# Sliding-window attention with global tokens and a top-k mixture of experts: blocks of 64 queries, heads in quads, grouped selection, one-hot inversion

## The chip, the cores and the metric

The kernel is one program on one core of a Trainium2 chip. Its time is the device time of one launch in microseconds (us). The kernel before took 876.09 us, the median of three runs (876.02, 876.09, 879.5).

The engines have their names from the profile: PE is TensorE, DVE is VectorE, ACT is ScalarE, POOL is GpSimd, SP is SyncE. POOL and SP also issue DMA transfers. The profile gives TensorE's granted clock as a share of full speed; its two levels are 0.5 (1.2 GHz) and 1.0 (2.4 GHz).

## The reference

Attention runs over 8 batches of 8 heads with 512 local and 32 global tokens and a head size of 64. Global queries see every token. A local query sees the 32 globals and the local keys at most 32 places away. The 4352 rows of 512 that come out go through a mixture of 8 experts: each row goes to its best expert, each expert keeps its 80 rows of highest gate, and every other row of the output is zero.

```python
out_g = softmax(scale * q_g @ k_all.T) @ v_all                     # global queries
s_ll  = where(abs(i - j) <= 32, scale * q_l @ k_l.T, -1e9)         # band
out_l = softmax(concat(scale * q_l @ k_g.T, s_ll)) @ concat(v_g, v_l)
x = concat(out_g, out_l) as (8 * 544, 512)
e = argmax(x @ w_gate);  gate = softmax(x @ w_gate)[e]
for each expert e: keep the 80 rows of e with the highest gate
    out[rows] = gate[rows] * (relu(x[rows] @ w1[e]) @ w2[e])       # 512 -> 1024 -> 512
```

## The kernel before

It has four stages, one after another.

**Attention, batch by batch, in pairs of heads.** Queries and keys come as fp16 by ten DMAs a batch on POOL's queue (L156 to L160), values as fp32 on SP's (L162). A pair is transposed on PE (L189, L191), copied by ACT (L194, L195), scored in blocks of 128 keys by 192 queries (L205; global queries L208, global keys L213, L215) and put through exp by ACT (L219 to L225). DVE multiplies by the band of zeros and ones (L227, 128x896 per head). In the product with the values, the 65 columns of a value block (64 and a column of ones for the denominator) are stationary, and the fp32 exponentials move through (L232, L235 for the globals; L240, L242): the result is `xTu`, 65 rows by tokens. It has to be turned round: ACT copies it (L247, L248), and PE multiplies it as the stationary operand with `wx`, an identity with the head's rows of the gate weights beside it (L251, L253). So `px` holds token rows, their denominators and their share of the gate logits; DVE divides and adds up (L256 to L272). Every fp32 matmul counts as two in the profile, a transpose as one.

**Selection.** After a batch its rows go to DRAM (`x_scr`, L277, L279). DVE makes gates and a one-hot score (L282 to L307), PE turns it to 8 experts x 640 tokens (L311), and ten rounds of MAX8 and MATCH_REPLACE (L318, L321) put the batch's 80 best per expert into `cand`. After the last batch ten more rounds over the 8x640 of `cand` (L332, L334) give each expert's threshold.

**Routing.** Every kept token gets its place, expert times 80 plus its rank among the kept (L337 to L401). 40 indirect DMAs on POOL's queue scatter token number and gate to those places in DRAM (`tokgate_scr`, L406).

**Experts.** For each expert: read back 80 numbers and gates (L416), gather 80 rows (L420), transpose (L424), first product with the rows stationary (L432), relu (L436, L437), transposes of the hidden rows (L442), second product (L448), gate (L451), scatter to the output (L453). The weights of experts 0 to 2 are loaded during attention; those of e+3 are issued on POOL's queue within expert e (L144, L146).

Each engine takes its instructions in the order of the program; a buffer in a pool is handed out again when its readers are done. `order` rows below show that order.

Of the kernel before, what the change touches and what calls it, by code (L numbers as in the profile page):

```python
# [18 lines left out]
P = 128  # L19
WIN = 32  # L20
QSTART = [0, 96, 224, 320]
NRND_B = 10
NRND_F = 10
WPREF = 3


def _np_consts(B, H, SL, SG, D, E, S, NT, cap):
    c = {}
    c["ident16"] = np.eye(P, dtype=np.float16)
    c["identf"] = np.eye(P, dtype=np.float32)  # L30
    m = np.zeros((P, 4, 224), dtype=np.float32)
    for j in range(4):
        p = np.arange(P)[:, None]
        col = np.arange(192)[None, :]
        q = QSTART[j] + col
        k = 128 * j + p
        m[:, j, 0:192] = (np.abs(q - k) <= WIN).astype(np.float32)
        m[:, j, 192:224] = 1.0
    c["band"] = m
    c["tri"] = (np.arange(P)[:, None] <= np.arange(P)[None, :]).astype(np.float32)  # L40
    tokid = np.full((P, NT), 2.0e9, dtype=np.float32)
    for b in range(B):
        for tau in range(4):
            tokid[:, b * 5 + tau] = b * S + SG + 128 * tau + np.arange(P)
        tokid[0:SG, b * 5 + 4] = b * S + np.arange(SG)
    c["tokid"] = tokid
    e80 = np.zeros((1, E, NT), dtype=np.float32)
    for e in range(E):
        e80[0, e, :] = e * cap
    c["e80"] = e80  # L50
    wxc = np.zeros((65, H, 73), dtype=np.float32)
    wxc[64, :, 8] = 1.0
    for h in range(H):
        wxc[0:64, h, 9:73] = np.eye(64, dtype=np.float32)
    c["wxc"] = wxc
    c["ones_row"] = np.ones((1, P), dtype=np.float32)
    return c
# [3 lines left out]
def kernel(  # L61
# [22 lines left out]
    NT = B * 5  # L84
    cap = int(moe_capacity)
    scale = float(1.0 / np.sqrt(D))
    assert SL == 512 and SG == 32 and D == 64 and P == 128 and DF == H * D

    c = _np_consts(B, H, SL, SG, D, E, S, NT, cap)
    ident16_d = nc.inline_tensor(c["ident16"], name="cident16")  # L90
    identf_d = nc.inline_tensor(c["identf"], name="cidentf")
    band_d = nc.inline_tensor(c["band"], name="cband")
    tri_d = nc.inline_tensor(c["tri"], name="ctri")
    tokid_d = nc.inline_tensor(c["tokid"], name="ctokid")
    e80_d = nc.inline_tensor(c["e80"], name="ce80")
    wxc_d = nc.inline_tensor(c["wxc"], name="cwxc")
    ones_row_d = nc.inline_tensor(c["ones_row"], name="cones_row")

    x_dram = nc.dram_tensor("x_scr", (N, DF), BF16, kind="Internal")
    tg_dram = nc.dram_tensor("tokgate_scr", (E * cap, 2), FP32, kind="Internal")  # L100

    cpool = ctx.enter_context(tc.tile_pool(name="consts", bufs=1))
    gpool = ctx.enter_context(tc.tile_pool(name="glob", bufs=1))
    wpool = ctx.enter_context(tc.tile_pool(name="wpool", bufs=WPREF))

    ident16 = cpool.tile([P, P], FP16, name="ident16")
    nc.sync.dma_start(out=ident16, in_=ident16_d.ap())
    identf = cpool.tile([P, P], FP32, name="identf")
    nc.sync.dma_start(out=identf, in_=identf_d.ap())
    identbf = cpool.tile([P, P], BF16, name="identbf")  # L110
    nc.gpsimd.dma_start(out=identbf, in_=identf_d.ap())
    band = cpool.tile([P, 4, 224], FP32, name="band")
    nc.sync.dma_start(out=band, in_=band_d.ap())
    tri = cpool.tile([P, P], BF16, name="tri")
    nc.gpsimd.dma_start(out=tri, in_=tri_d.ap())
    tokidt = cpool.tile([P, NT], FP32, name="tokidt")
    nc.sync.dma_start(out=tokidt, in_=tokid_d.ap())
    e80t = cpool.tile([1, E, NT], FP32, name="e80t")
    nc.sync.dma_start(out=e80t, in_=e80_d.ap())
    ones_row = cpool.tile([1, P], FP32, name="ones_row")  # L120
    nc.sync.dma_start(out=ones_row, in_=ones_row_d.ap())
    wx = cpool.tile([65, H, 73], FP32, name="wx")
    nc.sync.dma_start(out=wx, in_=wxc_d.ap())
    nc.sync.dma_start(out=wx[0:64, :, 0:8], in_=moe_w_gate.rearrange("(h d) e -> d h e", d=64))

    zt = gpool.tile([P, DF], FP32, name="zt")
    nc.vector.memset(zt, 0.0)
    out_t = out.rearrange("(t p) d -> t p d", p=P)
    ztg = gpool.tile([P, (E * cap // P) * 2], FP32, name="ztg")
    nc.vector.memset(ztg, 0.0)  # L130
    nc.sync.dma_start(out=tg_dram.ap().rearrange("(a p) c -> p a c", p=P), in_=ztg)

    score_all = gpool.tile([P, E, NT], FP32, name="score_all")
    gate_all = gpool.tile([P, NT], FP32, name="gate_all")
    nc.vector.memset(score_all, 0.0)
    nc.vector.memset(gate_all, 0.0)
    cand = gpool.tile([E, B, 8 * NRND_B], FP32, name="cand")

    w1sb = {}
    w2sb = {}  # L140
# [7 lines left out]
    with tc.tile_pool(name="battn", bufs=2) as bpool, \  # L148
# [4 lines left out]
        def load_batch(bb):  # L153
# [14 lines left out]
            bt[bb] = (qk16, qkg16, vb, vgb)  # L168

        load_batch(0)  # L170
        for b in range(B):
            if b + 1 < B:
                load_batch(b + 1)
            if b == 1:
# [315 lines left out]
```

## Time and profile before

| what | value |
|---|---|
| median of three runs | 876.09 us |
| profiled execution: span | 878.1 us |
| PE busy | 505.7 us, 58% |
| DVE busy | 326.9 us, 37% |
| ACT busy | 174.9 us, 20% |
| POOL busy | 134.2 us, 15% |
| DMA, mean | 58 GB/s |

The span of the profiled execution is taken as its own time; it is 2.0 us above the median of the runs. Busy shares are means over four stages with different limits, so a stage is read from its own window and from the chain of work that ended last.

### The profile page before, as it was taken

The numbers are of one execution on the slowest core, as the hardware profiler recorded it, in microseconds if no ns is written. First come the engines' busy times: TensorE is split into PE (matmuls) and PEld (weight loads), VectorE is DVE, ScalarE is ACT, GpSimd is POOL, SyncE is SP. The second block draws the span as 40 slices with busy tenths as digits, with TensorE's granted clock in tenths as the row PEclk, the third lists the DMA queues.
The fourth block names the chain that finished last, engine by engine and source line by source line (L and its number), as shares of the span: only waits on it lengthen the run. The fifth ranks groups of instructions, "written<-read, shape, count | busy, mean of one in ns | idle before, by whom it ended". The sixth has DMA issues, their size and how long they took to land.

```text
span 878.1 us, 8534 instructions
## 1 busy us (share of the span) xinstructions
PE 505.7 (58%) x3151; PEld 332.0 (38%) x3151; DVE 326.9 (37%) x1125; ACT 174.9 (20%) x441; POOL 134.2 (15%) x158
## 2 busy tenths in 40 slices
PE   0477868776886777788668688867401000025255
PEld 0354546544554544565445466444300000012122
DVE  0032472375256328425733823652696000001011
ACT  0133222332222323222242222323000000000001
POOL 4412000300300030030011000000000433332221
PEclk9975666665656666566665657656555555558587
DMA  9999900900730090083019000000000000009791
GB/s 203 223 272 226 139 1 1 104 25 1 51 78 1 1 128 0 1 55 74 1 11 116 1 1 1 26 1 1 25 0 0 0 0 0 0 12 182 140 186 50
DMA packets 108956, 51.35 MB, mean 58 GB/s; under 512 B 78767, under 2 KB 99761, under 8 KB 108914
## 3 DMA queue, kind: packets, MB, share of 16 engines
q0 software_dynamic: 85920, 27.75, 28.2%
q1 hardware_dynamic: 18098, 14.13, 7.2%
q10 hardware_dynamic: 4896, 8.92, 3.3%
q8 instruction: 25, 0.41, 0.2%
q14 instruction: 17, 0.14, 0.1%
HBM read 61.83 MB, written 14.73 MB: 87 GB/s over the span
## 4 chain that ended last, share of the span: by engine, by line
PE 48%; DVE 17%; ACT 10%; DMA 9%; issue 9%; POOL 5%; POOLq 0%; ACTq 0%; SPq 0%; DVEq 0%
PE xTu_ps L240 18%; PE xTu_ps L232 7%; PE px_ps L251 7%; DVE scT L321 5%; DVE mx L318 5%; POOL tokgate_scr L406 4%; DMA out_dram<-ysb,idxu 4%; PE xgu_ps L242 4%; ACT qkT L194 3%; ACT eL L219 3%; PE qkT_ps L189 3%; DMA qk<-in_k_l_dram 2%; DMA xg<-x_scr,idxu 2%; PE scL_ps L205 2%; PE px_ps L253 2%
## 5 line engine op out<-in xcount | busy, mean ns | idle before, releaser
L240 PE MATMUL xTu_ps<-eL,vb 128*65 128x192 f32 x512 | 196.8, 500 | 19.9 <-DVE eL L227 19.9
L242 PEld LDWEIGHTS xgu_ps<-eL,vb 128*65 128x65 f32 x512 | 104.9, 208 | 35.7
L232 PE MATMUL xTu_ps<-eG,vgb 32*65 32x512 f32 x128 | 76.7, 1082 | 65.7 <-ACT eG L225 65.7
L227 DVE TENSOR_TENSOR eL<-eL,band 128x896 f32<-128x896 f32 x64 | 67.7, 1081 | 87.5 <-ACT eL L219 87.5
L247 ACT COPY xTu<-xTu_ps 65x512 f32<-65x512 f32 x64 | 36.9, 585 | 272.4 <-PE xgu_ps L242 227.4
L240 PEld LDWEIGHTS xTu_ps<-eL,vb 128*65 128x65 f32 x512 | 80.5, 212 | 24.0 <-DVE eL L227 21.7
L156 POOL DMA_DIRECT2D qk<-in_q_l_dram x32 | 29.1, 908 | 364.7 <-PE qkTg_ps L191 359.3
L242 PE MATMUL xgu_ps<-eL,vb 128*65 128x32 f32 x512 | 84.4, 258 | 0.0
L256 DVE RECIPROCAL rden<-px_ps 128x4 f32<-128x4 f32 x64 | 11.6, 180 | 192.1 <-PE px_ps L253 190.7
L424 PE MATMUL xgT_ps<-identbf,xg 80*128 80x80 bf16 x32 | 3.3, 248 | 135.3 <-DMA xg<-x_scr,idxu 135.3
L406 POOL DMA_INDIRECT tokgate_scr<-vals,dest_u x40 | 38.9, 973 | 273.4 <-DVE dest_u L401 212.2
L251 PE MATMUL px_ps<-wx,xTu 65*128 65x73 f32 x512 | 71.2, 282 | 5.0 <-ACT xTu L247 4.8
L219 ACT ACTIVATE eL<-scL_ps 128x448 f32<-128x448 f32 x128 | 62.3, 533 | 52.8 <-PE scL_ps L215 28.7
L251 PEld LDWEIGHTS px_ps<-wx,xTu 65*128 65x128 f32 x512 | 62.1, 191 | 11.2 <-ACT xTu L247 7.8
L318 DVE MAX8 mx<-scT 8x8 f32<-8x640 f32 x80 | 64.8, 810 | 0.8
L321 DVE MATCH_REPLACE8 scT<-mx,scT 8x640 f32<-8x640 f32 x72 | 57.4, 797 | 0.0
L424 PEld LDWEIGHTS <-xg 80*128 80x128 bf16 x32 | 2.2, 126 | 137.5 <-issue 113.0
L194 ACT COPY qkT<-qkT_ps 128x1024 f16<-128x1024 f16 x32 | 32.4, 1012 | 109.4 <-PE qkT_ps L189 109.4
L418 DVE CAST idxu<-tg 80x1 uint32<-80x1 f32 x8 | 1.2, 150 | 141.6 <-DMA tg<-tokgate_scr 104.9
L436 ACT ACTIVATE hsb<-hps 80x512 bf16<-80x512 f32 x8 | 4.7, 593 | 232.9 <-PE hps L432 232.9
L189 PE MATMUL qkT_ps<-ident,qk 128*128 128x128 f16 x256 | 32.3, 262 | 29.2 <-DMA qk<-in_q_l_dram 28.8
L232 PEld LDWEIGHTS xTu_ps<-eG,vgb 32*65 32x65 f32 x128 | 11.4, 203 | 79.0 <-ACT eG L225 78.7
(112 smaller groups left out, 588.5 us busy)
## 6 DMA issues: line engine op xcount, KB each, us to landing
out_dram<-zt ACTq DMA_DIRECT2D x34, 256.0 KB, 8.6
w1sb<-in_moe_w_dram POOLq DMA_DIRECT2D x8, 1024.0 KB, 15.1
w2sb<-in_moe_w_dram POOLq DMA_DIRECT2D x8, 1024.0 KB, 18.0
qk<-in_q_l_dram POOLq DMA_DIRECT2D x32, 128.0 KB, 4.4
qk<-in_k_l_dram POOLq DMA_DIRECT2D x32, 128.0 KB, 4.9
x_scr<-xsb SPq DMA_DIRECT2D x32, 128.0 KB, 3.0
tokgate_scr<-vals,dest_u POOLq DMA_INDIRECT x40, 2.1
vgb<-in_v_g_dram SPq DMA_DIRECT2D x8, 64.0 KB, 4.4
```

Of the source, the lines that this page charges most:

```text
L189: nc.tensor.transpose(out=qkT_ps[:, t, 128 * i:128 * (i + 1)], in_=qk16[:, t, i, hA:hA + 2, :], identity=ident16[:, :])
L194: nc.scalar.copy(out=qkT[:, :, 0:SL], in_=qkT_ps[:, :, :])
L219: nc.scalar.activation(out=eL[hh][:, 2 * jj:2 * jj + 2, :], in_=scL2[hh][jj][:, :, 0:224], func=AF.Exp, scale=scale)
L227: nc.vector.tensor_tensor(out=eL[hh][:], in0=eL[hh][:], in1=band[:], op=ALU.mult)
L232: nc.tensor.matmul(out=xTu_ps[hh][:, :], lhsT=vgb[32 * hh:32 * hh + 32, pr, :], rhs=eG[32 * hh:32 * hh + 32, 0:SL], start=True, stop=False)
L240: nc.tensor.matmul(out=xTu_ps[hh][:, QSTART[j]:QSTART[j] + 192], lhsT=vj, rhs=eL[hh][:, j, 0:192], start=False, stop=(j == 3))
L242: nc.tensor.matmul(out=xgu_ps[hh][:, :], lhsT=vj, rhs=eL[hh][:, j, 192:224], start=False, stop=(j == 3))
L247: nc.scalar.copy(out=xTu[:, 0:SL], in_=xTu_ps[hh][:, :])
L251: nc.tensor.matmul(out=px_ps[:, tau, :], lhsT=xTu[:, 128 * tau:128 * (tau + 1)], rhs=wx[:, h, :], start=True, stop=True)
L318: nc.vector.max(out=mx8[:], in_=scT[:])
L321: nc.vector.match_replace(out=scT[:], in_to_replace=mx8[:], in_values=scT[:], imm_value=0.0)
L406: nc.gpsimd.indirect_dma_start(out=tg_dram.ap(), out_offset=bass.IndirectOffsetOnAxis(ap=dest_u[:, t:t + 1], axis=0), in_=vals[:, t, :], i ...
```

## The change

Everything between the loads and the output is written anew.

**Attention.** The unit is a quad of 4 heads (16 quads, two a batch), loaded by two DMAs (`load_qk`) and put in order by DVE (`regroup`). `T_chunk` transposes two heads; POOL puts the global keys beside the local ones. `S_chunk` scores blocks of 64 queries against the 128 keys that their window can touch; for odd blocks the two halves of the keys are written separately, so that each lies where its values are. Half of the band products (128x512) are DVE's, half POOL's. `G_chunk`, `H_chunk` and `Q_chunk` take the exponentials as the stationary operand and the 65 columns of the values as the moving one, so token rows come out at once: no `xTu`, no `px`. POOL writes a second copy of each batch's values, shifted by 64 rows (`spread_v`). The normalised rows are transposed (`X_chunk`) for the gate logits (`L_chunk`, 20 fp32 matmuls a batch); POOL casts them to bf16 for DRAM, with the gate behind each row. The chunks of quad q+1 are written between those of quad q.

**Selection.** `K_chunk` works on groups of 4, 3 and 1 batches. The first two run ten rounds on 40 rows (5 slices of tokens x 8 experts) of 512 or 384, and ten on the 8x400 that are left; the two results are merged by one maximum. The last batch joins without rounds of its own, and ten rounds on 8x720 give the threshold.

**Routing.** Ranks come from a scan and two matmuls; 40 matmuls with one-hot columns (rank j of token row) give an 80x8 table of token numbers. The 40 scatters and the read-back are gone; 8 gathers and 8 scatters use the table.

**Experts.** The hidden layer comes out transposed (w1 stationary, 80 columns moving), so its transposes go. The weights of experts 3 to 7 have buffers of their own, in space that the attention pools give back.

```diff
-    nc.tensor.matmul(out=xTu_ps[hh][:, QSTART[j]:QSTART[j] + 192], lhsT=vj, rhs=eL[hh][:, j, 0:192], ...)
-    nc.tensor.matmul(out=px_ps[:, tau, :], lhsT=xTu[:, 128 * tau:128 * (tau + 1)], rhs=wx[:, h, :], ...)
...
+    def spread_v(b):
+        nc.gpsimd.tensor_copy(out=v[0:64, 5:9], in_=v[0:64, 1:5])
+        nc.gpsimd.tensor_copy(out=v[64:128, 5:9], in_=v[64:128, 0:4])
...
+        for t in range(0, 8, 2):                                   # S_chunk
+            for hh in range(2):
+                nc.tensor.matmul(out=l_ps[hh][:, 64 * t:64 * t + 64],
+                                 lhsT=buf[o:o + 64, 512 + 64 * t:640 + 64 * t],
+                                 rhs=buf[o:o + 64, 64 * t:64 * t + 64], start=True, stop=True)
...
+            nc.scalar.activation(out=eL[:], in_=l_ps[hh][:], func=AF.Exp, scale=scale)
+            eng = nc.vector if hh == 0 else nc.gpsimd
+            eng.tensor_tensor(out=eL[:], in0=eL[:], in1=band[:].rearrange("p t i -> p (t i)"), op=ALU.mult)
...
+                nc.tensor.matmul(out=s["o"][h][:, u, :], lhsT=s["eG"][r, 128 * u:128 * u + 128],   # G_chunk
+                                 rhs=vgb[r, b, qd, :], start=(u == 0), stop=False,
...
+                nc.tensor.matmul(out=o[64 * odd:64 * odd + 64, u, :], lhsT=s["eL"][h][:, 64 * t:64 * t + 64],   # H_chunk
+                                 rhs=v[:, 5 * odd + u, hd, :], start=False, stop=(u == 3),
...
+                nc.tensor.matmul(out=lg[:, u, :], lhsT=bs["xT"][cc][:, 128 * u:128 * u + 128],   # L_chunk
+                                 rhs=wg[:, cc, :], start=(cc == 0), stop=(cc == 3))
...
+        top_rounds(scT[:], lst[:])                                 # K_chunk
+        for s in range(NB):
+            nc.sync.dma_start(out=cand[:, s, :], in_=lst[8 * s:8 * s + 8, :])
+        top_rounds(cand[:].rearrange("e s r -> e (s r)"), R[g][:])
...
+    for q in range(NQ):
+        if q + 2 < NQ:
+            load_qk(q + 2)
...
+        T_chunk(q + 1, 0)
+        G_chunk(q)
+        H_chunk(q, 0)
+        T_chunk(q + 1, 1)
+        H_chunk(q, 1)
+        S_chunk(q + 1, 0)
+            g = L_chunk(pending)
+                K_chunk(g)
+        H_chunk(q, 2)
+        X_chunk(q, 0)
+        S_chunk(q + 1, 1)
+        H_chunk(q, 3)
+        Q_chunk(q)
+        X_chunk(q, 1)
...
+    astack.close()
+    for e in range(NRES, E):
+        load_w(e, w2pool, bufs=E - NRES)
...
+        nc.vector.tensor_tensor(out=OH[i][:], in0=iota1[:].unsqueeze(1).to_broadcast([P, 10, cap]),
+                                in1=jt[:, 10 * i:10 * i + 10].unsqueeze(2).to_broadcast([P, 10, cap]),
+                                op=ALU.is_equal)
+        for t in range(10):
+            nc.tensor.matmul(out=inv_ps[:].rearrange("j e k -> j (e k)"), lhsT=OH[i][:, t, :],
+                             rhs=rv[:, 10 * i + t].rearrange("p e k -> p (e k)"),
...
+    for e in range(E):
+        nc.gpsimd.indirect_dma_start(out=xg[e][:], out_offset=None, in_=x_dram.ap(),
+                                     in_offset=bass.IndirectOffsetOnAxis(ap=idx[:, e:e + 1], axis=0),
```

On PE, before, a pair ends like this: the last value products (`xTu_ps`, `xgu_ps`), the turning round (`px_ps`), and only then the transposes of the next pair (`qkT_ps`).

```order
L240 MATMUL xTu_ps_194<-eL_162,vb_114 65x192
L242 MATMUL xgu_ps_196<-eL_162,vb_114 65x32
L251 MATMUL px_ps_220<-wx,xTu 128x73 x4
L253 MATMUL px_ps_220<-wx,xTu 32x73
L251 MATMUL px_ps_239<-wx,xTu 128x73 x4
L253 MATMUL px_ps_239<-wx,xTu 32x73
L189 LDWEIGHTS qk_0_102
L189 MATMUL qkT_ps<-ident_64,qk_0_102 128x128
```

In the changed kernel the same engine, in the middle of a quad (`lg` gate logits of the batch before, `o_ps_2` and `o_ps_3` outputs of this quad's third and fourth heads, `G_ps` and `l_ps` scores of the next quad):

```order
L354 MATMUL lg_2420<-wgq,xgT 32x8 x4
L302 MATMUL o_ps_2_2319<-vb_88,eL_1_0_2241 64x65 x7
L241 LDWEIGHTS kbd
L241 MATMUL G_ps_2373<-qkT_121,kbd 64x512
L302 MATMUL o_ps_3_2320<-vb_88,eL_1_1_2244 64x65
L258 LDWEIGHTS qkT_120
L258 MATMUL l_ps_0_1_2385<-qkT_120 128x64
```

Scores of the next quad now stand between the value products of this one.

On DVE, before, the rounds of a batch (`mx`, `scT`) stand between band products (L227) and the divisions of the next batch's pairs:

```order
L227 TENSOR_TENSOR eL_716<-eL_716,band 128x896
L319 COPY cand<-mx_632 8x8
L321 MATCH_REPLACE scT<-mx_632,scT 8x640
L318 MAX mx_632<-scT 8x8
L319 COPY cand<-mx_632 8x8
L321 MATCH_REPLACE scT<-mx_632,scT 8x640
L256 RECIPROCAL rden<-px_ps_774 128x4
L318 MAX mx_632<-scT 8x8
```

In the changed kernel the rounds of a group do, after the fourth and the seventh batch alone:

```order
L412 MAX lst<-scT_923 40x8
L336 COPY xT_0_2536<-x_ps_0_2531 128x512
L414 MATCH_REPLACE scT_923<-lst,scT_923 40x512
L323 RECIPROCAL rg<-og_2591 128x1
L336 COPY xT_1_2620<-x_ps_1_2615 128x512
L412 MAX lst<-scT_923 40x8
L324 TENSOR_SCALAR xgn_2315<-og_2591,rg 128x64
L414 MATCH_REPLACE scT_923<-lst,scT_923 40x512
L306 RECIPROCAL rec<-o_ps_0_2645 128x4
```

One round now covers four (or three) batches, with one attention instruction after each step.

On POOL's queue, before, the end of attention is followed by the 40 scatters, three gathers, and then weights and scatters in turn:

```order
L406 DMA tokgate_scr<-vals,dest_u 640x2 x40
L420 DMA xg<-x_scr,idxu 80x512 x3
L144 DMA w1sb_4736<-in_moe_w_dram 128x4x1024
L146 DMA w2sb_4738<-in_moe_w_dram 128x8x512
L453 DMA out_dram<-ysb,idxu 4352x512
```

In the changed kernel ten weight loads come first (the last two are shown), then two small products (`rv`), then the eight gathers, of which two are shown:

```order
L439 DMA w1sb_4396<-in_moe_w_dram 128x4x1024
L441 DMA w2sb_4398<-in_moe_w_dram 128x8x512
L553 TENSOR_TENSOR rv<-keep,aw 128x320
L555 TENSOR_TENSOR rv<-keep,prow 128x320
L584 DMA xg_4513<-x_scr,idx 80x257
L584 DMA xg_4514<-x_scr,idx 80x257
```

All eight gathers stand behind all ten weight loads, and the scatters of the output behind the gathers.

## Rows read from the trace of the kernel before

**Rows 1.** The page: span; busy time, share and count of each engine.

```profile
span 878.1 us, 8534 instructions
PE 505.7 (58%) x3151; PEld 332.0 (38%) x3151; DVE 326.9 (37%) x1125; ACT 174.9 (20%) x441; POOL 134.2 (15%) x158
```

**Rows 2.** Windows by stage: length, busy per engine, PEclk, DMA share, GB/s.

```profile
0.00:31.00 31.00, 1.76 (x8) 0.76 (x8) 1.14 (x10) 1.31 (x2) 14.21 (x22) 1.00 1.45 199
31.00:623.00 592.00, 454.02 (x2907) 307.15 (x2907) 264.82 (x953) 164.39 (x423) 57.63 (x71) 0.65 0.38 54
623.00:647.00 24.00, 1.23 (x5) 0.47 (x5) 21.80 (x63) 0.24 (x1) 0.00 (x0) 0.50 0.07 23
647.00:677.00 30.00, 2.97 (x7) 1.25 (x7) 25.58 (x69) 0.00 (x0) 0.00 (x0) 0.50 0.00 0
677.00:779.00 102.00, 0.00 (x0) 0.00 (x0) 0.00 (x0) 0.00 (x0) 38.92 (x40) 0.50 0.01 0
779.00:878.00 99.00, 45.77 (x224) 22.36 (x224) 13.56 (x32) 8.94 (x16) 23.47 (x26) 0.71 0.70 126
812.00:824.00 12.00, 0.00 (x0) 0.00 (x0) 0.15 (x1) 0.00 (x0) 2.81 (x3) 0.57 1.20 219
```

**Rows 3.** Chain that ended last, start to 40: start, us, what.

```profile
8.91 21.68 DMA qk<-in_k_l_dram
```

**Rows 4.** Timeline of PE at clock 1.0: start, us, what.

```profile
264.50 0.52 PE L240 MATMUL xTu_ps<-eL,vb 128*65 128x192 f32 x2
264.86 0.25 PE L242 MATMUL xgu_ps<-eL,vb 128*65 128x32 f32 x2
264.94 1.09 PE L251 MATMUL px_ps<-wx,xTu 65*128 65x73 f32 x8
265.97 0.31 PE L253 MATMUL px_ps<-wx,xTu 65*32 65x73 f32 x2
267.50 0.40 PE L189 MATMUL qkT_ps<-ident,qk 128*128 128x128 f16 x4
267.83 0.18 PE L191 MATMUL qkTg_ps<-ident,qkg 32*128 32x32 f16 x1
```

**Rows 5.** Timeline of PE at clock 0.5, scores of a pair.

```profile
215.59 0.34 PE L205 MATMUL scL_ps<-qkT 64*128 64x192 f16 x2 [0.97 <-ACT qkT L194]
216.45 0.61 PE L213 MATMUL scG_ps<-qkT 64*32 64x512 f16 x2
216.85 0.24 PE L215 MATMUL scL_ps<-qkT 64*32 64x32 f16 x2
```

**Rows 6.** Chain, from the last batch to the scatters.

```profile
622.43 0.31 PE px_ps L253 x2
...
627.24 0.83 DVE mx L318
...
663.49 1.34 DVE keep L348 x8
...
677.32 1.06 POOL tokgate_scr L406
```

**Rows 7.** Chain, experts.

```profile
781.74 2.56 DMA xg<-x_scr,idxu
...
819.00 8.59 DMA xg<-x_scr,idxu
...
868.54 2.60 DMA out_dram<-ysb,idxu
```

**Rows 8.** Groups of instructions by line and shape: count, busy, mean ns.

```profile
L227 DVE TENSOR_TENSOR eL<-eL,band 128x896 f32<-128x896 f32 x64 | 67.7, 1081 | 87.5 <-ACT eL L219 87.5
L318 DVE MAX8 mx<-scT 8x8 f32<-8x640 f32 x80 | 64.8, 810 | 0.8
L219 ACT ACTIVATE eL<-scL_ps 128x448 f32<-128x448 f32 x128 | 62.3, 533 | 52.8 <-PE scL_ps L215 28.7 <-PE scL_ps L208 24.0
L321 DVE MATCH_REPLACE8 scT<-mx,scT 8x640 f32<-8x640 f32 x72 | 57.4, 797 | 0.0
```

More of the change, by code (lines that the diff above doesn't have):

```diff
@@ new lines, with psT @@
+    assert cap == 8 * NRND and E == 8
+    c = _np_consts(B, S, SG, cap)
+    cd = {k: nc.inline_tensor(v, name="c" + k) for k, v in c.items()}
+    x_dram = nc.dram_tensor("x_scr", (N, XW), FP32, kind="Internal")
+    cpool = ctx.enter_context(tc.tile_pool(name="consts", bufs=1))
+    wpool = ctx.enter_context(tc.tile_pool(name="wpool", bufs=NRES))
+    ps = ctx.enter_context(tc.tile_pool(name="psum", bufs=2, space=bass.MemoryType.PSUM))
+    def psT(shape, dt, name):
+        return ps.tile(shape, dt, tag="T", bufs=2, name=name)
@@ new lines, in X_chunk @@
+    def X_chunk(q, j):
+        b, qd = divmod(q, 2)
+        s = st[q]
+        bs = bst[b]
+        x_ps = psT([P, 512], FP32, f"x_ps{q}_{j}")
+        for u in range(4):
+            nc.tensor.transpose(out=x_ps[:, 128 * u:128 * u + 128],
+                                in_=s["xn"][:, u, 128 * j:128 * j + 128], identity=identf[:, :])
+        xT = hpool.tile([P, 512], FP32, tag="xT", bufs=5, name=f"xT{q}_{j}")
+        nc.vector.tensor_copy(out=xT[:], in_=x_ps[:])
+        bs["xT"].append(xT)
+        if j == 1:
+            nc.gpsimd.tensor_copy(out=bs["xb"][:, :, 128 * qd:128 * qd + 128].bitcast(BF16), in_=s["xn"][:])
@@ new lines @@
+    regroup(0)
+    setup_globals(0)
+    T_chunk(0, 0)
+    T_chunk(0, 1)
+    spread_v(0)
+    S_chunk(0, 0)
+    S_chunk(0, 1)
+    pending = None
+    for q in range(NQ):
+        b, qd = divmod(q, 2)
+        nxt = q + 1 < NQ
+        if qd == 0 and b + 1 < B:
+            load_v(b + 1)
+        if q + 2 < NQ:
+            load_qk(q + 2)
+        if q == 1:
+            setup_globals(1)
+        if qd == 1 and b < NRES:
+            load_w(b, wpool)
+        if qd == 1 and b >= 1:
+            zeros(3)
+        if nxt:
+            regroup(q + 1)
+        if nxt:
+            T_chunk(q + 1, 0)
+        G_chunk(q)
+        H_chunk(q, 0)
+        if nxt:
+            T_chunk(q + 1, 1)
+        if qd == 1 and b + 1 < B:
+            spread_v(b + 1)
+        H_chunk(q, 1)
+        if nxt:
+            S_chunk(q + 1, 0)
+        if pending is not None:
+            g = L_chunk(pending)
+            if g is not None:
+                K_chunk(g)
+            pending = None
+        H_chunk(q, 2)
+        X_chunk(q, 0)
+        if nxt:
+            S_chunk(q + 1, 1)
+        H_chunk(q, 3)
+        Q_chunk(q)
+        X_chunk(q, 1)
+        st.pop(q)
+        if qd == 1:
+            pending = b
@@ new lines @@
+    for e in range(E):
+        xT_ps = psT([P, 4, cap], BF16, f"xT_ps{e}")
+        for cc in range(4):
+            nc.tensor.transpose(out=xT_ps[:, cc, :], in_=xg[e][:, 64 * cc:64 * cc + 64].bitcast(BF16),
+                                identity=identbf[0:cap, 0:cap])
+        xT = rpool.tile([P, 4, cap], BF16, tag="fxT", bufs=2)
+        nc.vector.tensor_copy(out=xT[:], in_=xT_ps[:])
+        hT = rpool.tile([P, 8, cap], BF16, tag="fhT", bufs=2)
+        for half in range(2):
+            h_ps = psO([P, 4, cap], FP32, f"h_ps{e}{half}")
+            for f in range(4):
```

751 lines of the change are left out of this document (381 added, 370 removed).

## The prediction

> **What bounds the kernel now.** I read the page's busy line first, then windows cut where the work changes, then the chain of waits inside each window, then PE's timeline. The busy line names no bound: PE is busy for 505.7 of 878.1 us, DVE for 326.9 [rows 1]. The windows do [rows 2]. From 31 to 623 PE is busy for 454 of 592 us at a mean clock of 0.65; with levels of 0.5 and 1.0 this is 1.0 for 30% of the stage. So attention is bound by PE, mostly at its lower clock, and the 138 us in which PE waits are what it spends between a pair's scores, exp, band product and value product. From 623 to 677 only DVE works: last selection and routing (47 us busy of 54). From 677 to 779 nothing computes: 40 scatters leave one at a time, 102 us. From 779 to 878 it is DMA: weights at 219 GB/s in the window 812 to 824, in which PE does nothing. Before all that stand 31 us of loads; one key load needs 21.68 us to land [rows 3]. This execution's span is 2.0 us above the median; I add up in its time and take 2 off at the end.
>
> **The change part by part.**
>
> *One quad on PE.* Prices at clock 1.0, from the starts in one stretch [rows 4]: two fp32 records with 32 moving columns take 0.08 us (264.86 to 264.94), 40 ns each; two with 192 take 0.36, 180 ns each; eight with 73 moving columns and 128 stationary ones take 1.03 (264.94 to 265.97), 129 ns each; four fp16 transposes take 0.33, 82 ns each. At clock 0.5 sixteen score matmuls take 0.86 us (54 ns each) and two with 512 columns 0.40 [rows 5]; I halve these. No row has 65 moving columns. Along the line from 32 to 192 columns it is 69 ns; the bounds are 40 and 129. I take 69, because the stationary block has 64 columns or fewer in most of them, as the 32- and 192-column rows have 65.
> - H_chunk: 32 matmuls, 64 records, 4.4 us. Q_chunk: 20, 40 records, 2.8 us. G_chunk: 16, 32 records, 2.2 us. Together 136 records, 9.4 us (5.4 to 17.5).
> - T_chunk: 16 x 82 ns = 1.3 us. S_chunk: 58 small matmuls x 27 ns = 1.6 us, two of 512 columns 0.2 us.
> - X_chunk: 8 transposes at the price of the 128-column record, 1.0 us. L_chunk: 40 records a batch x 129 ns = 5.2 us, 2.6 a quad.
>
> The sum is 16.1 us at clock 1.0 (12.1 to 24.2), 32 at 0.5; before, a quad's worth took 592 / 16 = 37 us. For the clock I take a mean of 0.85, since the scores of the next quad now stand between the value products of this one and the long gaps in which PE idled (138 us) have work written into them; a mean of 0.65 as before is a rival below. 16.1 / 0.85 = 19 us, and 1 us for waits that stay (the scores have two PSUM buffers, one held by the global block): 20 us a quad.
>
> G_chunk's stationary block has 32 rows and 128 columns. The rows price 128 columns at 129 ns, with 65 rows [rows 4]; no row here has 32 rows by 128 columns. The Trainium skill (TensorE: Matmul & The Clock Gate, section LDWEIGHTS) says that a load takes its columns divided by 1.2 a nanosecond, and that 32 rows take as long as 128; by that one such load is 107 ns, the trace's 129 agrees roughly, and G_chunk would be an estimated 3.4 us rather than 2.2. It speaks against turning the operands round: 1.2 us a quad, 23 us in all at clock 0.85.
>
> *The other engines in a quad.* ACT: a 128x448 exp is 533 ns [rows 8]; four of 512, one of 512 and two of 320 are 3.8 us, four copies of 512 at the same price 2.4: 6 of 20 us. DVE: band product 1081 ns for 896 elements, 1.21 ns each [rows 8]; two of 512 are 1.2 us, regroup, X copies and divisions, about 4100 elements at that price or less, at most 5.0, a batch's small operations 1.3: under 8 us. The rounds add to four quads of the first group and two of the second: 19 on 512 and 19 on 400 elements, at 810 ns per 640 for MAX8 and 797 for MATCH_REPLACE8 [rows 8], 22 us, some 5 a quad. Still under 20, so PE hides DVE. POOL: 4128 elements per partition in a quad (two band products, cast, half the batch's spread), and two DMA issues. The trace has no such operation on POOL, as its 57.63 us in attention are DMA issues but for small fills [rows 2]. Bounds: nothing gained or lost on the chain, if it stays under 20 us a quad, which it does up to 4.4 ns per element; above, each further nanosecond costs 4.1 us a quad. I take DVE's 1.21 as the nearest row, 5 us, and hide it behind PE.
>
> The Trainium skill (GPSIMD Engine Reference, section 3.1 Elementwise — side-by-side cycle accounting) has a two-input fp32 operation 1.96 times slower on GpSimd than on VectorE. No row here shows it; by it POOL's quad is an estimated 10 us, still behind PE.
>
> *Loads at the start.* First quad's queries and keys, values and constants, some 2.8 MB at 199 GB/s [rows 2], 14 us, then a first transpose-score-exp chain of 10: attention runs from 24 us. The last quad has no next one: 3 us less. It ends at 24 + 16 x 20 - 3 = 341 us. Three weight sets and the zeros move during attention as before, at 54 GB/s [rows 2], a quarter of what the loads at the start reach, and are not counted.
>
> *Selection's tail.* From the last value work to the first round took 4.5 us (622.74 to 627.24 [rows 6]); the logits' 40 records now come after it, 5.2: 10 us. DVE's queue then still holds the second half of the group of three: 19 rounds on 400 elements, 11 us with its DMAs' waits (up to 16). Both are in the program ahead of the release of the attention pools, on which weights 3 to 7 wait: they start at 341 + 10 + 11 = 362. The final rounds on 8x720 are 10 x 0.91 + 9 x 0.90 us = 17.3, 18 with loads. Routing took 14 us before, from threshold to first scatter (663.49 to 677.32 [rows 6]), with two dozen operations in a row; about ten now, one of them 128x800 and four times, 11 us. So the table of tokens stands at 362 + 29 = 391.
>
> *Experts.* The 40 scatters go with their 102 us, and the read-back. But eight gathers stand behind ten weight loads on POOL's queue. Each is 1.05 MB, at 219 GB/s 4.8 us [rows 2]: 48 us, to 410. A gather behind weights landed with them before: 8.59 us instead of 2.56 [rows 7]. So the first gather lands at about 413, 22 us later than the table allows. By then all weights are there, and experts run back to back: PE's 45.77 us in this stage are 5.7 per expert at a clock of 0.71 [rows 2]; without the hidden rows' transposes and the waits between, 4.4 (3.7 to 7), 35 us: 448. From the last scatter's start to the end of the span were 9.6 us (868.54 to 878.1 [rows 1, 7]): 458, less 2 for the execution: 455 after rounding. What follows attention is thus 117 us of span instead of 255.
>
> **The rivals.**
>
> *Quads run at full clock, tiles side by side* (0.17). The 64-column blocks overlap in the array, 40 ns a record, and PE never cools: 12.1 us of work, 15 a quad with waits: 80 us less, 375. For it: 192 columns in 180 ns, faster than 73 in 129 per column, so something already overlaps. Against: the small matmuls need 5 times as many loads per product as before.
>
> *The clock stays as before* (0.15). At 0.65 a quad is 16.1 / 0.65 + 1 = 26 us: 96 more, 551. For it: PE was busy for 77% of the stage before and the mean was 0.65 all the same; 16.1 of 20 us is 80%. Against: the gaps are now shorter. *PE stays at 0.5* or the records cost 129 ns (0.10): 33 us a quad, 663.
>
> *The gathers are not held up by the weights* (within the main case): 22 us less, 433.
>
> *POOL binds, slower than before* (0.01). Its 4128 elements a quad decide from 4.4 ns each; the kernel gets slower than before at (878 - 117 - 24 + 3) / 16 = 46 us a quad, less 1.8 for DMA issue 44 us, 10.7 ns per element, nine times DVE's price. It would give 880 or more. For it: no POOL row of this size; against: the factor.
>
> **How the numbers follow.** The main case (0.57) has its own range of 415 to 500 (a quad of 18 to 22.5 us, gathers held or not): 455. With full clock 0.17 (360 to 415, half of it below 395), the old clock 0.15 (500 to 560), the low clock 0.10, POOL 0.01. From 395 to 560 about 0.19 is left out. A measurement of this kernel can tell 0.5% from no change, 4 us; no case but POOL's lies near or above 876: faster 0.985, same 0.005, slower 0.01.
>
> **What would show it.** Right: quads repeat every 18 to 22 us, PE busy for over 85% of attention with a mean clock above 0.8, POOL busy for under 10 us in each; the first gather lands with the last weight load, 20 us after the table; no gap in the experts. Wrong: an H_chunk record near 129 ns or a clock near 0.65 (too short by 100 us); POOL or the exps of ACT ahead of every value product on the chain; a gather that lands ahead of the weights; DVE's rounds holding divisions, so that quads 8 to 11 take visibly longer.

## The result, and the profile after

The changed kernel takes 452.65 us, the median of five runs (447.5 to 464.2), against 877.14 before: a ratio of 0.5125 (0.5096 to 0.5154). Forecast were 455, from 395 to 560. The time of one kernel varies by some 4% with the clock that its execution got (a listed mean of 0.677 in the longest run, 0.73 in one of the shortest), so a ratio is taken over the faster executions, and differences under 3% between kernels are read from their traces here.

The page of the profiled execution (span 450.9, so 1.75 below its time), beside [rows 1]:

```profile
span 450.9 us, 10118 instructions
PE 332.3 (74%) x4268; PEld 271.3 (60%) x4268; DVE 212.5 (47%) x558; ACT 142.5 (32%) x201; POOL 173.8 (39%) x248
PEclk9999956598579569578658555895565555555999
```

Its windows, cut where the work changes, with the columns of [rows 2]:

```profile
0.00:30.00 30.00, 9.75 (x100) 6.70 (x100) 12.69 (x26) 10.24 (x13) 18.11 (x29) 1.00 1.27 168
30.00:327.00 297.00, 279.44 (x3730) 232.70 (x3724) 145.66 (x414) 125.08 (x173) 124.38 (x175) 0.71 0.56 113
327.00:339.50 12.50, 9.02 (x49) 8.25 (x48) 5.68 (x17) 0.00 (x0) 5.24 (x15) 0.63 0.17 24
339.50:358.50 19.00, 0.50 (x3) 0.11 (x2) 15.26 (x45) 0.24 (x1) 0.26 (x3) 0.50 0.09 29
358.50:387.00 28.50, 4.75 (x44) 3.60 (x44) 25.19 (x42) 0.00 (x0) 10.67 (x12) 0.50 1.10 190
387.00:413.50 26.50, 0.09 (x2) 0.09 (x3) 0.00 (x0) 0.00 (x0) 7.11 (x8) 0.50 1.18 213
413.50:451.00 37.50, 28.78 (x352) 19.83 (x352) 8.00 (x16) 6.99 (x16) 8.04 (x9) 0.91 0.13 39
```

Attention went from 592 to 297 us, and all behind it from 255 to 124. PE is busy for 94% of attention, where it was 77%, but its mean clock is hardly above that of before: the view has 0.71 beside 0.65. Both are a little too high. The profile's first clock record stands at 47.0 us, and the view counts the time ahead of it as 1.0; but a record of L302 lasts 320 ns there, as at 0.5 (323 ns from 108.6 to 128.9) and not as at 1.0 (231 ns from 91.5 to 108.4). With that time at 0.5 the means are 0.68 and 0.64. Means of attention's clock in the text below are corrected like this, and the lines of the views are as they came. From 387 to 413.5 nothing computes: gathers wait behind weights at 213 GB/s. The same wait on POOL's queue, beside [rows 7] (start, us, what, idle before and its releaser):

```profile
387.06 1.07 POOL L584 DMA_INDIRECT xg<-x_scr,idx  x1 [6.60 <-DVE idx L577]
...
413.23 0.96 POOL L584 DMA_INDIRECT xg<-x_scr,idx  x1 [4.20 <-DMA w2sb<-in_moe_w_dram]
420.68 0.96 POOL L610 DMA_INDIRECT out_dram<-y,idx  x1 [6.49 <-DVE y L608]
```

The first gather, issued at 387.06, landed at 413.4, the last weight load at 413.0.

What a quad costs at either clock can be read from two stretches of attention at 1.0 and the two at 0.5 behind them:

```profile
91.40:108.40 17.00, 14.65 (x268) 12.12 (x266) 7.96 (x21) 11.18 (x15) 10.44 (x19) 1.00 1.07 167
108.50:128.90 20.40, 19.78 (x233) 16.33 (x234) 9.77 (x26) 6.54 (x10) 11.86 (x16) 0.50 1.04 212
129.00:146.00 17.00, 15.10 (x271) 12.66 (x269) 6.55 (x19) 10.45 (x15) 8.39 (x15) 1.00 1.16 163
146.10:166.40 20.30, 20.17 (x235) 16.48 (x236) 10.12 (x28) 8.21 (x12) 9.44 (x13) 0.50 0.46 145
```

A quad has 3730 / 16 = 233 records. At 63 ns each (17.0 / 268) it takes 14.7 us at clock 1.0, at 87 ns (20.4 / 233) 20.4 us at 0.5. But these stretches hold unlike work: the two at 1.0 have 21 and 26 records of the wide logit products (L351), the two at 0.5 have 13 and 7, and PE waits for 2.3 and 1.9 us in the former, for 0.6 and 0.1 in the latter. So I also took each line's price over all of attention, from a record's start to the next record's, waits left out, and summed it over a quad's records: an estimate of 13.9 us at 1.0 and 22.1 at 0.5, 1.6 times. The band's records (L302) cost 51 and 70 ns, those of the logits 117 and 224.

### The profile page after: what moved, and what is told of

The parts are those of the page before. It is cut to its first block, busy times and chain, and to the rows that moved or that the text cites. A ratio compares the mean times of both kernels' runs of the same rounds, so it can differ in the third digit from the quotient of the medians.

```text
span 450.9 us, 10118 instructions
## 1 busy us (share of the span) xinstructions
PE 332.3 (74%) x4268; PEld 271.3 (60%) x4268; DVE 212.5 (47%) x558; ACT 142.5 (32%) x201; POOL 173.8 (39%) x248
## 5 line engine op out<-in xcount | busy, mean ns | idle before, releaser
L227 ACT COPY qkT<-T_ps 128x512 f16<-128x512 f16 x64 | 77.7, 1369 | 94.0 <-PE T_ps L222 94.0
L273 POOL TENSOR_TENSOR eL<-eL,band 128x512 f32<-128x512 f32 x32 | 42.3, 1321 | 80.6 <-ACT eL L271 70.2
L302 PE MATMUL o_ps<-vb,eL 128*64 128x65 f32 x1024 | 70.2, 281 | 0.1
L302 PEld LDWEIGHTS o_ps<-vb,eL 128*64 128x64 f32 x1024 | 55.3, 184 | 9.4 <-issue 3.1
L271 ACT ACTIVATE eL<-l_ps 128x512 f32<-128x512 f32 x64 | 37.0, 600 | 60.6 <-PE l_ps L266 59.0
L289 PE MATMUL o_ps<-vgb,eG 32*128 32x65 f32 x512 | 52.6, 363 | 0.9 <-DVE xgn L324 0.7
L351 PE MATMUL lg<-wg,xT 128*128 128x8 f32 x256 | 46.2, 318 | 5.8 <-ACT qkT L227 5.3
L289 PEld LDWEIGHTS o_ps<-vgb,eG 32*128 32x128 f32 x512 | 45.8, 263 | 7.5 <-issue 4.8
L351 PEld LDWEIGHTS lg<-wg,xT 128*128 128x128 f32 x256 | 44.7, 271 | 7.5 <-ACT qkT L227 6.0
L217 POOL COPY qkT<-kbd 64x32 f16<-64x32 f16 x64 | 16.1, 251 | 55.4 <-PE l_ps L258 43.3
L333 PE MATMUL x_ps<-identf,xn 128*128 128x128 f32 x128 | 28.6, 366 | 2.9 <-DVE xn L307 2.2
```

The source lines that it names most:

```text
L227: eng(out=dst[:, t].rearrange("x (p i) -> x i p", i=4), in_=T_ps[:, t].rearrange("x (i p) -> x i p", i=4))
L271: nc.scalar.activation(out=eL[:], in_=l_ps[hh][:], func=AF.Exp, scale=scale)
L273: eng.tensor_tensor(out=eL[:], in0=eL[:], in1=band[:].rearrange("p t i -> p (t i)"), op=ALU.mult)
L289: nc.tensor.matmul(out=s["o"][h][:, u, :], lhsT=s["eG"][r, 128 * u:128 * u + 128], rhs=vgb[r, b, qd, :], start=(u == 0), stop=False, skip_ ...
L302: nc.tensor.matmul(out=o[64 * odd:64 * odd + 64, u, :], lhsT=s["eL"][h][:, 64 * t:64 * t + 64], rhs=v[:, 5 * odd + u, hd, :], start=False, ...
L333: nc.tensor.transpose(out=x_ps[:, 128 * u:128 * u + 128], in_=s["xn"][:, u, 128 * j:128 * j + 128], identity=identf[:, :])
```

## The experiments

The edits are to the changed kernel, but for one that says otherwise. Each time is a median.

### The tail: who holds the gathers

**Gathers behind six loads.** The loop that loads experts 6 and 7 moves behind the gathers:

```diff
-    for e in range(NRES, E):
+    for e in range(NRES, NRES + 3):
         load_w(e, w2pool, bufs=E - NRES)
...
+    for e in range(NRES + 3, E):          # behind the eight gathers
+        load_w(e, w2pool, bufs=E - NRES)
```

> The eight gathers are issued behind six of the ten late weight loads instead of behind all ten; the other four loads follow the gathers. Theory: the gathers wait only because they stand behind the weights. In the changed kernel the table of tokens stands at 386.8, the first gather is issued at 387.1 and lands at 413.4, with the last weights. With six loads ahead (29 us at 4.8 each from 358) it should land at about 391, the experts run from there at 3.7 us each, and the last four loads (20 us) land by about 412, just ahead of expert 6: some 20 us less, 430 to 435 us. Rival: the wait moves to the weights of experts 6 and 7 or to the queue's semaphores, and the end stays within 1% (over 447).

447.25 us (440.7 to 465.7). Two of the four loads were placed ahead of the gathers again, and the first gather landed at 401.0, right behind the eighth load (400.6): a gather lands with what stands ahead of it. But of 12 us, 2 of which came from an earlier start of the loads (356.3), only 7 reached the end (span 444.0).

**Held by data.** Now the last four loads can't go ahead:

```diff
+        for w, src in ((w1sb[e], moe_w1), (w2sb[e], moe_w2)):     # e = 6, 7, behind the gathers
+            nc.vector.tensor_copy(out=w[0:cap, 0, 0:1], in_=idx[:, 0:1])
+            nc.gpsimd.dma_start(out=w[:], in_=src[e].rearrange("(c p) f -> p c f", p=P))
```

> Six late weight loads ahead of the gathers and four behind them, and this time those four can't be moved ahead: each of their buffers is first touched by a one-column copy of the table of tokens. (In the run before, two of the four were placed ahead of the gathers again, eight loads in all, and the gathers landed at 401 with the eighth.) Theory: a gather lands with the last load that stands ahead of it. Six loads from 356 land at 387 to 390, the gathers at about 392, experts at 3.9 us each, the last four loads by about 418, in time for experts 6 and 7: 428 to 434 us. Rival: the experts then wait for their own weights, or the landing is set by something else; over 441.

455.1 us (452.7 to 462.3), the rival's side. The gathers landed at 396.1, 17 us earlier. Then, on POOL's queue and on DVE:

```profile
404.28 0.99 POOL L617 DMA_INDIRECT out_dram<-y,idx  x1 [0.82 <-DVE y L615]
425.88 0.95 POOL L617 DMA_INDIRECT out_dram<-y,idx  x1 [20.61 <-issue]
```

```profile
425.18 0.75 DVE L615 TENSOR_SCALAR y<-y_ps,xg 80x512 f32<-80x512 f32 x1 [10.82 <-DMA out_dram<-y,idx]
```

The first scatter stands behind the four loads in the same queue, the next waits for its landing (20.61 us), and DVE and then PE wait for its buffer. Gathers or scatters, something small always stands behind the weights. The last load lands at 423.6 here and at 413.0 in the changed kernel, and both executions end at 450.9.

**Lists of the rounds apart.** So start the loads earlier. They wait for the attention pools, and with them for the second half of the group of three:

```diff
-            bst["scT"] = lpool.tile(...)
+            bst["scT"] = cpool.tile(...)
-        lst = lpool.tile(...)
+        lst = cpool.tile(...)
-        cand = lpool.tile(...)
+        cand = cpool.tile(...)
```

> The tiles of the grouped rounds move to a pool that stays, so the late weights wait for the attention pools without the second half of the group of three. Theory: the loads start at about 343, when the last batch's scores are made, instead of 358; ten of them take 49 us and land at 392, the gathers (issued at 387) with them: 430 to 436 us. Rival: another reader holds the space until 355 or later, or the loads delay the small transfers of the lists by as much: over 443.

449.29 us (438.95 to 454.6); the profiled execution (454.6) had a slower attention, so its trace is read from the end of the logits: the loads start 9.4 us behind them (350.2 to 359.6) instead of 19.1 (339.4 to 358.5), and the wait from table to first gather is 17.2 us instead of 26.8. The time is on the rival's side (over 443). The loads gain 10 of the 15 us expected: the last batch's rows lie in that space too, and their transfer to DRAM (355.24) landed at 358.65, one us before the first load.

### Attention: engines beside PE

**Band products on DVE alone.**

```diff
-            eng = nc.vector if hh == 0 else nc.gpsimd
+            eng = nc.vector
```

> All band products (128x512) go to VectorE, none to GpSimd. Theory: both engines hide behind TensorE, which is busy for 93% of attention: VectorE goes from 151 to about 177 us busy of 303, GpSimd from 130 to 87, and the time stays within 1.5% of 452 us. Rival: GpSimd's slower product (1.32 us against 0.82) holds the value products of every second head, and without it attention is 3% or more shorter (under 440). Third: VectorE is late with its divisions and holds PSUM, over 460.

473.07 us (467.1 to 477.5), the third case: 20 us slower. PE's wait for the divisions, at the transposes of X_chunk, with this kernel's row first and the changed kernel's below:

```profile
L333 PE MATMUL x_ps<-identf,xn 128*128 128x128 f32 x128 | 32.5, 388 | 15.3 <-DVE xn L307 9.8 <-DVE rec L306 4.8 <-DVE scT L406 0.6
```

```profile
L333 PE MATMUL x_ps<-identf,xn 128*128 128x128 f32 x128 | 28.6, 366 | 2.9 <-DVE xn L307 2.2 <-DVE scT L406 0.6
```

12 us more of waits, and a mean clock in attention of 0.64 instead of 0.68. DVE was busy for half of the stage only (156.83 of 322 us); it is late all the same, since it works in order and a 0.73 us product can stand ahead of a division.

**One round instead of ten** in both halves of the first two groups (another selection):

```diff
-        top_rounds(scT[:], lst[:])
+        top_rounds(scT[:], lst[:], 1)
-        top_rounds(cand[:].rearrange("e s r -> e (s r)"), R[g][:])
+        top_rounds(cand[:].rearrange("e s r -> e (s r)"), R[g][:], 1)
```

> Of the ten rounds on the group of four and of the ten on the group of three, and of the ten on the lists of each, only the first is made (the selection is not the reference's; the final rounds and all that follows stay). In the changed kernel two quads take 36.3 us, but 40.9 and 50 in the two batches beside the rounds of the first group. Theory: the rounds hold up VectorE's divisions, so that TensorE waits there: some 18 us come back in attention and 11 to 12 in the tail (second half of the group of three), 418 to 428 us. Rival, as in the prediction: TensorE hides the rounds in attention, only the tail gets shorter: 438 to 443.

427.69 us (422.75 to 431.3), 25 less, as the theory had it. Between the starts of the global scores, the two batches beside the first group's rounds took 37.0 and 37.4 us instead of 40.9 and 50.0, 16.5 less; a stretch of 65 us at clock 0.5 from there on took most of that back, so that of the 22 us between the two profiled executions 5 lie in attention and 17 in the tail. But the theory's reason is not what the traces show: PE idles for 5.9 us in these two batches with the rounds and for 6.6 without. What differs is the price of the products with the globals, 17.5 us for 9.0. With the rounds they were placed eight at a time, without them in longer runs (the changed kernel's rows first, at clock 1.0 and at 0.5, then this one's at 1.0):

```profile
208.47 1.10 PE L289 MATMUL o_ps<-vgb,eG 32*128 32x65 f32 x8
...
254.76 1.97 PE L289 MATMUL o_ps<-vgb,eG 32*128 32x65 f32 x8
```

```profile
211.36 1.07 PE L289 MATMUL o_ps<-vgb,eG 32*128 32x65 f32 x18 [0.69 <-DVE xgn L324]
```

137 ns against 59 at clock 1.0. Eight records are what one head has, on the same 32 rows of the array; the profile does not name the head, but at clock 0.5 such an eight takes 1.97 us, exactly what one head's eight take in the kernel with turned operands below. So about half of the 16.5 us is, by this reading, the order in which PE's work was placed beside the rounds; why it was placed so is not shown. The rest goes with the clock of these batches (0.75 and 0.57 with the rounds, 0.77 and 0.68 without).

**Without interleaving.** The chunks of quad q+1 are written behind all of quad q:

```diff
         Q_chunk(q)
         X_chunk(q, 1)
+        T_chunk(q + 1, 0); T_chunk(q + 1, 1)       # these four stood between G, H and Q above
+        S_chunk(q + 1, 0); S_chunk(q + 1, 1)
```

> The transposes and scores of quad q+1 are written behind all work of quad q instead of between its chunks; instructions and their number stay. Theory: the interleaving hides the way from a transpose over the copies on ScalarE (1.37 us each, four a quad), scores, exp and band product to the first value product; written apart it leaves TensorE idle for 6 to 8 us a quad, about 110 us, and the clock falls further: 540 to 600 us. Rival: the gain over the kernel before comes from the turned operands alone (less work a quad), engines run ahead by themselves, and the time stays under 480.

469.74 us (469.5 to 472.6): 17 more, not 110. Attention takes 328 us with PE busy for 271 of them: it idles 57 instead of 18. The mean clock is 0.66 instead of 0.68. ACT and the score buffers work ahead enough in this order too. My theory of what interleaving gives falls.

### Attention: prices on PE

**Globals twice.**

```diff
+        for u in range(4):                      # the loop of G_chunk a second time
+            for h in range(4):
+                nc.tensor.matmul(out=s["o"][h][:, u, :], lhsT=s["eG"][r, 128 * u:128 * u + 128],
+                                 rhs=vgb[r, b, qd, :], start=False, stop=False, ...)
```

> The products with the global values (32 rows x 128 columns stationary, 65 moving) are issued twice, so the globals count double in the output; 256 more matmuls, 512 more records. Theory of the prediction: 69 ns a record at clock 1.0, TensorE bound: 35 to 45 us more, 485 to 495. Second: priced by the 128 columns, 107 ns or more a record, 55 to 65 us more, 505 to 515. Rival: TensorE is not what bounds a quad, the doubling hides: under 465.

484.38 us (477.95 to 493.1); 31.7 us more for 512 records, 62 ns each at a mean clock of 0.66. In the trace the added records (the second loop's) cost 50 ns at clock 1.0 and 81 at 0.5. PE bounds a quad; of the two prices the first is nearer, though 69 ns at clock 1.0 is too high, and 107 ns is out.

**The turned operands alone, in the kernel before.** Its scores, selection, routing and experts stay:

```diff
+                    for tau in range(4):
+                        nc.tensor.matmul(out=o_ps[:, tau, :], lhsT=eG[g0, 128 * tau:128 * tau + 128],
+                                         rhs=vgb[g0, pr, :], start=(tau == 0), stop=False, ...)
+                    for j, tau, p0, c0, n in PIECES:         # ten pieces of 128, 64 or 32 queries
+                        nc.tensor.matmul(out=o_ps[p0:p0 + n, tau, :], lhsT=eL[hh][:, j, c0:c0 + n],
+                                         rhs=vb[:, h, j, :], start=False, stop=(j == 3), ...)
```

> The kernel before with one part of the change: the exponentials are the stationary operand of the value products (per head 4 pieces for the globals, 10 for the band, 5 for the global queries), so token rows come out; the turning round by wx goes, and the logits come from transposed rows (20 fp32 matmuls a batch and 20 transposes). Scores, selection, routing and experts stay. Theory: TensorE's work a pair goes from some 18.5 us to 13 (411 us of start-to-start time in these products before, 76 records a pair at 60 to 70 ns and 2.3 us of transposes and logits after), and attention from 592 to about 420: 690 to 730 us. Rival: the chain within a pair (transposes, copies, scores, exp, band product) sets the pace as soon as the products are shorter, and the clock stays lower: 760 or more.

1061.99 us (1055.7 to 1068.2), a ratio of 1.208 to the kernel before: 183 us slower, where I had expected 160 faster. The page's clock and the chain of waits in a pair:

```profile
PEclk9999855555555555555555555555555555556778
```

```profile
369.93 1.97 PE o_ps L241 x8
...
373.71 4.38 PE o_ps L247 x20
378.09 1.00 PE og_ps L251 x8
```

Eight records with the globals stationary take 1.97 us, 246 ns each, twenty of the band 4.38, 219 each, and eight of 32 columns 1.00, 125 each, and the clock stays at 0.5. Turning the operands by itself is not what made attention faster. The 9s at the left of the clock's line are no measurement: the first clock record stands at 118.9 us, and the globals' records last as long ahead of it as behind it (420 and 424 ns). One execution of this kernel, without a trace, is listed with a mean clock of 0.979 and yet is the longest of the four, 1068.16 us; such a mean is not to be trusted.

**Neighbours on the same part of the array.** In the changed kernel itself, the three inner loops the other way round:

```diff
-        for u in range(4):
-            for h in range(4):
+        for h in range(4):                      # G_chunk; H_chunk and Q_chunk alike
+            for u in range(4):
                 r = slice(32 * h, 32 * h + 32)
```

> The changed kernel with the three inner loops of the value products turned over, nothing else: the globals head by head (same 32 rows of the array four times in a row) instead of tile by tile, the band products first all even blocks and then all odd ones (same 64 columns) instead of in turn, the global queries head by head (same 32 columns) instead of key block by key block. Same instructions, same number. Theory: the changed kernel's products are cheap because neighbours use different rows or columns of the array and run side by side (start to start at clock 0.5: 94, 59 and 28 ns in it, but 227, 205 and 109 ns in the run with turned operands in the old kernel, where neighbours use the same ones). At these prices a quad gets 32 x 133 + 64 x 146 + 40 x 81 ns = 17 us longer at clock 0.5, less at 1.0: 640 to 740 us. Rival: the price follows the columns of the stationary block alone (64 or 32 instead of 128), whatever the order: 445 to 480.

482.62 us (479.2 to 486.2): 30 more, neither case. The mechanism is there, at a smaller price. The globals of a quad at clock 1.0 and the global queries at 0.5, in this kernel:

```profile
110.71 2.82 PE L289 MATMUL o_ps<-vgb,eG 32*128 32x65 f32 x32
...
106.05 2.83 PE L317 MATMUL og<-vb,eQ 128*32 128x65 f32 x36
```

and in the changed one, at the same clocks:

```profile
100.43 1.83 PE L289 MATMUL o_ps<-vgb,eG 32*128 32x65 f32 x31
...
117.77 1.30 PE L317 MATMUL og<-vb,eQ 128*32 128x65 f32 x38
```

88 ns against 59 and 79 against 34: the same records come closer together when their neighbours lie on other rows or columns of the array. That the loss is 30 us and not 190 has two reasons in the traces. The prices that I had carried over were those of the other kernel, with other pieces: at clock 0.5, from a record's start to the next record's, globals, band and global queries cost 177, 96 and 85 ns here and 112, 70 and 42 in the changed kernel. And the mean clock in attention rose from 0.68 to 0.74.

Summed over a quad at clock 0.5, the value products take 31 us in the old kernel with turned operands, 15.2 here and 9.8 in the changed kernel. The order of neighbours is the last step, 5.4 of 21 us. The larger one came with the pieces (for the band eight of 64 queries a head, instead of ten of 128, 64 and 32) and with what else differs between the two kernels; no run takes these apart. Over the whole of attention, value products and their turning round took 368 us of PE's time before and 136 now, and PE's waits 138 and 18; transposes, scores and logits cost 57 us more.

### The clock

**Logits with 64 moving columns.**

```diff
-    wg = cpool.tile([P, 4, E], FP32, name="wg")
+    wg = cpool.tile([P, 4, 64], FP32, name="wg")     # 56 columns of zeros
```

> The gate-logit products of the local rows get 64 moving columns instead of 8 (56 of them zeros); number of instructions, stationary blocks and results stay. Theory: the granted clock falls in these products (128 stationary columns, 8 moving) and stays low for 20 us after them; with fuller products it stays up, mean clock in attention from 0.71 to above 0.8, a quad from 18.9 towards 16.5 us, time 410 to 435. Rival: the products are only work: 64 columns hide behind the load of 128 stationary ones or add up to 0.06 us to each of 256 records; the clock stays at 0.71 and the time lies between 450 and 468.

447.44 us (446.3 to 448.6), just under the rival's range, and a clock of 0.70 in attention: the rival, as far as this tells.

**Gate weights stationary.**

```diff
-                nc.tensor.matmul(out=lg[:, u, :], lhsT=bs["xT"][cc][:, 128 * u:128 * u + 128],
-                                 rhs=wg[:, cc, :], start=(cc == 0), stop=(cc == 3))
+            nc.tensor.matmul(out=lgT_ps[:], lhsT=wg[:, cc, :], rhs=bs["xT"][cc][:],
+                             start=(cc == 0), stop=(cc == 3))
...
+            nc.tensor.transpose(out=lg[:, u, :], in_=lgT[:, 128 * u:128 * u + 128], identity=identf[0:E, 0:E])
```

> The logits of the local rows are made with the gate weights stationary (8 columns) and 512 rows moving, 4 matmuls a batch instead of 16, then turned by 4 small transposes. Theory: the clock falls in the stretch of logits, where 128 columns are loaded for 8 that move (7 of 11 falls begin there); without that stretch it stays up, mean above 0.78 and 415 to 435 us. Rival: the stretch is only work, 8 records of 512 columns cost what 32 of 8 did, the clock stays at 0.70 to 0.73 and the time at 443 to 455.

435.4 us (432.7 to 447.8), 17 less. At clock 1.0 the work of a batch is the same as before, 8 records at 465 ns for 32 at 117, so the gain is not less work. In the profiled execution the clock's mean in attention is 0.75 instead of 0.68. Of the falls of the clock in attention 2 of 11 begin in a stretch of logits, where 6 of 10 did; so, as far as one execution of each tells, this stretch is one place where the clock falls, and not the only one. But this execution is the longest of the five, and its attention ends when the changed kernel's does (last product at 326.7 and 326.5): PE waits for 41 us of it instead of 18, 22 of them for DVE's `sc_all`, the gates that stand among the rounds. The other executions left no trace.

**Both improvements.** Gate weights stationary and the lists apart:

> Gate weights stationary in the logits and the tiles of the rounds in a pool of their own, both together. Theory: the two gains lie in different stages, 12 to 17 us in attention and 8 to 10 us between the last scores and the first late weight load: 422 to 430 us. Rival: the earlier loads only wait behind the last rows' transfer, or the gain in the clock was chance: 436 or more.

428.01 us (422.9 to 432.4), a ratio of 0.4888 (0.4864 to 0.4911) to the kernel before, the fastest kernel here. Its attention:

```profile
30.00:311.00 281.00, 240.06 (x3597) 178.32 (x3595) 153.12 (x417) 124.73 (x173) 124.93 (x175) 0.83 0.59 119
```

16 us less than in the changed kernel, at a clock of 0.82 with the time ahead of the first record corrected. What is left in this kernel are PE's waits in attention, 41 us (281.00 less 240.06), 22 of them for DVE's `sc_all`, and 17 us without compute, 367 to 384, behind the weights.

## Why the prediction was right, and where it was not

The sum came out within 1%; several of its terms did not, and cancelled.

- *Loads at the start*, 24 us: first global product at 30.1. Six short.
- *A quad's work*, 16.1 us at clock 1.0: 13.9 by the sum over lines (14.7 with waits by the two stretches). The term that was too large are the value products, 6.8 us for 9.4, 50 ns a record for the 69 (78, 51 and 26 ns for globals, band and global queries). With the inner loops turned over they cost 66 ns, so 69 was near the price of a poor order. The 40 ns of the rival that I gave 0.17 were nearer: it alone had the tiles work side by side, and it was wrong on the clock.
- *The clock*, a mean of 0.85: 0.68. This step failed. So did its companion, that a quad takes twice as long at 0.5: 22.1 against 13.9 is 1.6 times. By my own rule 0.68 gives 16.1 / 0.68 + 1 = 25 us; a quad took 18.6 (297 / 16), of which 1.1 are waits, for the 1 that I had put. A clock that was too low and work that was too cheap, at either level, cancelled; that is luck. The rival "the clock stays as before" had the clock right and its 551 us wrong.
- *Why*: I put the clock's rise down to the interleaving. Undone, it costs 17 us, and the clock goes from 0.68 to 0.66.
- *The other engines hide behind PE*: not quite. The two batches beside the first group's rounds take 16 us longer, about half of it by the order of PE's products; PE's own waits did not grow. I had named longer quads there as a sign against me, put them down to held divisions and given them no price. ACT's four copies a quad were 1369 ns each instead of 0.6 us, and did hide. POOL's band product took 1321 ns, 2.6 ns an element, between my 1.21 and the limit of 4.4; it is no bound, and giving its work to DVE costs 20 us.
- *The tail* had the right mechanism, gathers that wait behind weights, but its first date is luck too. Weights start at 358.5 (362): attention ended 14 us early (327 for 341), and from there it took 31.5 us for 21, since the way from the logits to the first load was 19.1 us for 11. From then on it was right nearly step by step. The table stands at 386.8 (391), the first gather lands at 413.4 (413), with the last weights (413.0; ten loads took 54.5 us for 48), 27 us after the table (22). From there to the last scatter's issue it took 33 us (413.4 to 446.2) for 35, and from that to the end 4.7 for 9.6.
- *The Trainium skill* (TensorE: Matmul & The Clock Gate, section LDWEIGHTS) prices a load by its columns whatever its rows. That rows do not count the trace bears out: a load of 32x128 lasts 263 ns in the changed kernel, one of 128x128 (L351) 271. As the price of a product it fails here: 50 ns for an added product at clock 1.0 where 128 columns would take 107. With 263 ns a load and 50 between products, the loads of the four strips of 32 rows must overlap; in the run where one head's products follow each other on one strip they cost 88 ns at clock 1.0. For what the Trainium skill has (GPSIMD Engine Reference, section 3.1 Elementwise — side-by-side cycle accounting: 1.96 times VectorE), the trace agrees roughly: 1321 ns against 819 with both at work, 1.61 times, or 1.82 against the 727 of DVE alone.

What sets the clock stays open. It followed neither the busy share (94% at 0.68, 96% at 0.74 in the kernel with turned loops, 83% at 0.66 without interleaving) nor the moving columns of the logits.

## What to carry to other kernels

Turning the operands round decides little by itself: with one set of pieces it cost 183 us, with another it came with a kernel of half the time. Price small products in the order in which they will stand, not by their shape alone: the same records cost 59 or 88 ns by their neighbours, and the order that counts is the placed one, which need not be the loop's. A small transfer lands with the large ones ahead of it in its queue, so moving it forward only moves the wait to the next small one; start the large ones earlier. And a sum that comes out right is no proof of its terms: look at each.

## What the runs showed of the hardware

- The old kernel with turned operands stayed at clock 0.5 for nearly all of attention with PE busy for 88% of it (682 of 773 us), and the kernel before, busy for 77%, reached 1.0 again and again.
- DVE's 128x512 band product took 819 ns beside POOL's and 727 ns when POOL made none.
- At the lower clock the value products cost 1.4 to 1.6 times as much (band 51 and 70 ns, global queries 26 and 42), the logits with 128x128 stationary blocks 1.9 times (117 and 224).
- Eight records with the globals of one head, on one strip of 32 rows, take 1.97 us at clock 0.5 in the old kernel with turned operands, and groups of eight take as long in the changed one; with four strips in turn they come 59 ns apart at clock 1.0.
- Ahead of its first clock record (47.0 us in the changed kernel, 118.9 in the old one with turned operands) the profile counts the clock as 1.0; the records' lengths there are those of 0.5.
